# An adaLN block with a spectral filter on one core: turning transfers issued ahead of normalisations, shift weights and tables queued later, special filter rows turned in the row loop, the gather two groups sooner

## Chip, cores and metric

The kernel runs on one core of one Trainium2 chip. The metric is the device time of one execution in microseconds (us), as the median of several runs. Besides the timed runs there is one profiled execution; all places and durations inside the kernel come from that one, counted from the start of its span.

The engines are called PE (matrix multiplications; PEld is its loading of weights), DVE (vector), ACT (scalar), POOL (GpSimd) and SP (it only issues transfers). Each has its own instruction queue and works through it in order; they wait for one another by semaphores. Transfers issued from SP, ACT or POOL are carried out by 16 DMA engines.

## The reference

There are two sub-blocks on x of 2048 x 640, each with a layernorm that is shifted and scaled, and a gated addition. The six modulation vectors come from one row `c`.

```python
mod = (silu(c) @ w_mod).reshape(1, 6, 1, -1)     # w_mod: 640 x 3840
sa, ca, ga, sb, cb, gb = ...                     # its six slices

h = layernorm(x) * (1 + ca) + sa
y = irfft2(rfft2(h) * (w_r + 1j * w_i))          # filter: 2048 x 321, complex
x = x + ga * y
h = layernorm(x) * (1 + cb) + sb
x = x + gb * ((silu(h @ w_gate) * (h @ w_up)) @ w_down)   # hidden width 1728
```

Inputs and output are bf16. The Fourier transform runs over both dimensions, tokens (2048) and features (640).

## The kernel before

The kernel is one long function that writes the instructions out in order; nothing reorders them. The order of the Python lines is the order in each engine's queue. The transforms are done as matrix products with tables of cosines and sines.

**Loads (L260 to L291, on SP).** SP issues x in 128-token tiles (`load_x(i)` brings tiles 2i and 2i+1), the token table `M`, the scale weights `wm_ca`, the feature table `R` (`Rp`), the first half of the filter's rows (`load_w`, L282, into `Wt[:, 0]` for the imaginary and `Wt[:, 2]` for the real part), the shift weights `wm_sa` (L287), the table `Ktab` (L289) and 16 special rows of the filter (`Wrow`, L291). At most eight transfers use the eight semaphores in turn, so an issue waits for the landing of the eighth one before it.

**The turned filter half.** The filter's second half is needed with its rows in reverse order. `flip` (L278), on POOL's queue, copies it from one place in DRAM to another, row by row in reverse; SP loads the result (L465) when that copy has landed. There are two flips, for `A_w_i` (L425, behind the first normalisations) and `A_w_r` (L463, in the row loop at t = 0).

**The row loop (L447 to L482)** runs over t = 0 to 7, each with two token tiles. For a tile, DVE takes mean and variance (`bn`, L325), POOL raises to the power -1/2 (`rstd_of`, L340) and POOL or DVE normalises (`xhat`, L350 on DVE, L352 on POOL; `xpair` does two tiles). Two early tiles have their statistics from ACT (`act_stats`, `act_var`). PE does the token transform (`st_a`, L365), ACT evicts it (L368), PE does the feature transform (`st_b`, L374 and L376) with tables `Rs` that hold the scale 1 + ca (L436 to L443), and ACT or DVE evicts into A (`a_ev`, L380). The loop does the statistics of tiles 2t+6 and 2t+7 while it transforms tile pair t+1. At t = 0 SP's queue receives the two loads of the turned halves, `wm_r` part 0 (the weights of the gate ga, L466), and the tables `Kstab`, `RI` and `Htab` (L467 to L469).

**The shift** enters only few frequencies. `sp_sa` (L387) multiplies the shift weights with silu(c) on PE (25 small matmuls, helper `mod_cols`, L319), DVE copies the result (L390), POOL spreads it (L391 to L394); `sp_sums` (L397) sums it over the features (10 matmuls, L401) and DVE scales it into `SA` (L402). Both stand in the row loop, at t = 6 and t = 7.

**The filter stage (L494 to L765).** The feature frequencies l = 0 to 80 are worked on in 21 groups, most of four. A is transposed once per l: groups 0 to 4 on PE (`t2_pe`, L519), the others by four DMA transposes that SP issues (`t2_dma`, L500) for l = 1 to 15, 16 to 31, 32 to 47 and 64 to 79. Per group PE mixes the row classes (`mix`, L538), DVE multiplies with the filter in two products of three terms each (`prod`, L562), PE combines and turns (`stage_b`, L569), ACT evicts (L572), PE mixes back (`stage_c`, L594), ACT or DVE evicts (`evac`, L603). The middle term needs the sum of real and imaginary filter, which `wsum` (L385) makes on DVE or POOL for a range of columns, for each half of the rows (rk = 0 the direct, rk = 8 the turned half). The loop runs over g; in step g it issues mix and products of group g + 2 and the back end of group g and before.

**The special rows** (frequencies that are a multiple of 128, one row of the transposed groups) go a path of their own: the filter's special rows are reversed (`sp_w(0)`, ACT, L615) and transposed by PE (`sp_w(1)`, L622, copied by ACT, L624, summed by POOL, L625); `sp_gather` (L629, on POOL, at g = 8) collects the special row of all groups and adds `SA`, so it waits for all four DMA transposes; `sp_mm` (L638, L643, L647) and `sp_ev` at g = 10, 12 and 14 mix, multiply and mix back, with `Kstab` as the table. POOL then puts the row into place by two small transfers (L666, L667).

**Behind it** PE does the inverse token transform (`s1em`, L688, with `Htab`, whose second half POOL makes with signs from `Kstab`, L746) and the inverse feature transform (L1220, L1223, with `RI`, which POOL multiplies with the gate ga, L752), and then the second sub-block: L1049 and L1079 for gate and up, L927 and L950 for down.

Of the kernel before, what the change touches and what calls it, by code (L numbers as in the profile page):

```python
# [19 lines left out]
NL = 81  # L20
# [146 lines left out]
def adaln_block_kernel(ctx, tc, A_x, A_w_r, A_w_i, B_x, B_w_gate, B_w_up, B_w_down, c, w_mod, out):  # L167
# [69 lines left out]
    Kstab = rE.cut(32904, [578])  # L237
    wm_sa = rE.cut(34560, [NC5, D])

    psum = ctx.enter_context(tc.tile_pool(name="psum", bufs=1, space=bass.MemoryType.PSUM)).tile([P, 8, 512], F32, name="psum")  # L240
# [40 lines left out]
    def load_w(i, w):  # L281
        nc.sync.dma_start(Wt[:, i, 0:8, :], bass.AP(tensor=w.tensor, offset=w.offset + 321, ap=[[321, P], [256 * 321, 8], [1, 321]]))  # L282

    load_x(4, 4)
    load_w(0, A_w_i)
    load_w(2, A_w_r)
    nc.sync.dma_start(wm_sa[:], wm_v[:, :, 0:D])  # L287
    wm_m = wm_v[:, :, 2 * D:6 * D].rearrange("p k (i d) -> p k i d", i=4)
    nc.sync.dma_start(Ktab[:], K_dram)  # L289
    for i, w in ((0, A_w_i), (1, A_w_r)):  # L290
        nc.sync.dma_start(Wrow[:, i, :], w.rearrange("(k2 k1) l -> k2 k1 l", k1=P)[:, 0, :])  # L291


# [28 lines left out]
    if True:  # L322
# [44 lines left out]
        def ht_ev(t, lo=0, hi=NC5, eng=None):  # L367
            (eng or nc.scalar.copy)(HTs[t % 3][:, lo:hi], zA[:, lo:hi])  # L368
# [18 lines left out]
        def sp_sa():  # L387
            mps = psum[:, 3, 0:NC5]
# [5 lines left out]
            nc.gpsimd.tensor_copy(_rev(SL, 1024, [[1, 4], [132, 2], [16, 8]]),  # L394
                                  sa4[:].unsqueeze(2).unsqueeze(3).to_broadcast([P, 4, 2, 8]))

        def sp_sums():  # L397
            sps = psum[:, 3, 128:128 + NL]
# [13 lines left out]
        bn(1)  # L412
        rstd_of(0, 2)
        nc.vector.tensor_copy(sc_col[:], sc_f[:])
        bn(2)
# [8 lines left out]
        xhat(2, nc.vector)  # L424
        flip(A_w_i, Wflip[0])  # L425
        idle_pe(3)
        idle2(9)
        st_a(0)
        ht_ev(0)
        mps = psum[:, 3, 32:32 + 32 * NC5]  # L430
        mod_cols(mps, wm_ca, range(0, 3), 32)
# [10 lines left out]
        nc.vector.tensor_scalar_mul(Rs[:, 0, 2, :], Rp[:, 2, :], one_p_ca[:, 2:3])  # L442
        nc.vector.tensor_scalar_mul(Rs[:, 0, 3, :], Rp[:, 3, :], one_p_ca[:, 3:4])  # L443
        act_var(5)
        rstd_of(4, 2)
        on_dve = {(4, 1), (5, 1), (6, 1)}
        for t in range(8):  # L447
# [11 lines left out]
            if u < NT:  # L459
                bn(u + 1)  # L460
                rstd_of(u, 2)
                if t == 0:
                    flip(A_w_r, Wflip[1])  # L463
                    for i in range(2):
                        nc.sync.dma_start(Wt[:, 2 * i, 8:16, :], Wflip[i][:])  # L465
                    nc.sync.dma_start(wm_r[:, :, 0, :], wm_m[:, :, 0, :])  # L466
                    nc.sync.dma_start(Kstab[:], Ks_dram)  # L467
                    nc.sync.dma_start(RI[:], RI_dram)
                    nc.sync.dma_start(Htab.rearrange("p (t h) v k -> p t h (v k)", h=2)[:, :, 0, :], H_dram.rearrange("p t v k -> p t (v k)"))  # L469
            for ck in range(2):  # L470
# [7 lines left out]
            if t == 6:  # L478
                sp_sa()
                wsum(48, 64, 0, nc.vector)  # L480
            if t == 7:
                sp_sums()  # L482
        for ls in (slice(0, 48), slice(64, 81)):
# [9 lines left out]
    if True:  # L493
# [14 lines left out]
        t2_dma(2)  # L508
        t2_dma(3)
        nc.sync.dma_start(wm_r[:, :, 1:3, :], wm_m[:, :, 1:3, :])  # L510
        nc.sync.dma_start(wm_r[:, :, 3, :], wm_m[:, :, 3, :])
# [97 lines left out]
        Osp = rE.cut(21192, [80])  # L609
        Wrev = rE.cut(21352, [2, 322], parts=16)  # L610
        Wsp = rE.cut(22640, [3, 2, NT, 2], parts=81)

        def sp_w(part):
            if part == 0:
                nc.scalar.copy(Wrev[:, :, 0:321], _rev(Wrow, 320, [[321, 2], [-1, 321]]))  # L615
            elif part == 1:
                tp = psum[0:81, 3, 448:512].bitcast(BF16).rearrange("p (v h a k) -> p v h a k", v=2, h=2, a=2)
                for v in range(2):
                    for hl in range(2):
                        for a in range(2):  # L620
                            o = 160 * (1 - a if hl else a)
                            nc.tensor.transpose(tp[:, v, hl, a], (Wrev if hl else Wrow)[:, v, o:o + 81], identb[0:16, 0:16])  # L622
                for v in range(2):
                    nc.scalar.copy(Wsp[:, 2 * v].rearrange("p h k a -> p h a k"), tp[:, v])  # L624
                nc.gpsimd.tensor_tensor(Wsp[:, 1], Wsp[:, 0], Wsp[:, 2], ALU.add)  # L625

        def sp_gather():
# [86 lines left out]
        t2_pe(3)  # L714
        xps2 = mix(2)
        prod(2, xps2, 0)
        prod(2, xps2, 1)
        ga_mod(320, 3)
        stage_a(3)
        ga_mod(0, 3)  # L720
        for lo, hi in ((0, 16),):
            wsum(lo, hi, 0, nc.vector)
        sp_w(0)
        for rk in (0, 8):
            v = [_rev(Wt, WP * i + 321 * rk + 80, [[321, 8], [160, 2]]) for i in range(3)]
            nc.gpsimd.tensor_tensor(v[1], v[2], v[0], ALU.add)
        wsum(0, 16, 8, nc.gpsimd)
        sgn_H = Htab.rearrange("p (t h) v k -> p t h (v k)", h=2)
        for g in range(NG + 1):
            for lo, rk in {1: ((16, 0), (16, 8)), 4: ((32, 0), (32, 8)), 9: ((64, 0), (64, 8))}.get(g, ()):  # L730
                wsum(lo, lo + 16, rk, nc.gpsimd)
            if g == 3:
                sp_w(1)
            if g == 5:
                nc.gpsimd.tensor_copy(sgnc[:], Kstab[:, 576:577])
            if g == 8:
                sp_gather()
# [620 lines left out]
```

## Time and profile before

| | us |
|---|---|
| median of 3 timed runs | 253.17 (253.15 to 253.75) |
| profiled execution | 253.96 |
| its span, first to last instruction | 252.2 |
| PE busy in the span | 237.0 (94%) |
| DVE busy | 204.9 (81%) |
| ACT busy | 166.6 (66%) |
| POOL busy | 72.8 (29%) |

The granted clock of PE is 1.0 throughout. Places in time: the first `st_a` starts at 8.62 us, the last at 30.43; the first DMA transpose is issued at 36.25; the products of the filter stage run from 37.70; `s1em` starts at 67.02.

The profile is read from several views. The page gives busy time by engine, the busy share in 40 slices, and the groups of instructions with mean duration and with the idle time before them and what ended it. The chain of waits follows the last instruction back to what released it. The timeline lists instructions in order with start and duration. The windows give the busy time of each engine in a stretch, the granted clock, and in the last two columns the busy share of the DMA engines (it can pass 1, since it is a sum over packets that overlap) and what they moved. In all views `L352` is a line of the kernel before, `psum<-rE` is output and input, and rX, rM, rA, rE, rW, rH, rL and rY are regions of on-chip memory that several tensors share one after the other.

### The profile page before, as it was taken

What the parts mean: (1) busy time and instruction counts of PE and PEld (TensorE: products, weight loads), DVE (VectorE), ACT (ScalarE), POOL (GpSimd) and SP (SyncE); (2) the same over time, 40 slices, a digit from 0 to 9 for tenths busy, and PEclk for the clock granted to TensorE, in tenths of its full rate; (3) what the DMA queues carried; (4) which work ended last, traced back from release to release, by engine and by line L of the source; (5) the groups of instructions that cost most, each with busy time, mean ns of one, the idle gap of its engine ahead of it and who ended that gap; (6) DMA issues with size and microseconds to landing.
All of it is one profiled execution on the core that took longest, in us unless ns stands there. A gap on an engine that the chain in (4) does not pass through costs nothing.

```text
span 252.2 us, 5929 instructions
## 1 busy us (share of the span) xinstructions
PE 237.0 (94%) x2237; PEld 185.8 (74%) x2237; DVE 204.9 (81%) x494; ACT 166.6 (66%) x329; POOL 72.8 (29%) x104
## 2 busy tenths in 40 slices
PE   8668997979999999999999999999999999999994
PEld 3556875969889888778887778888775665656773
DVE  4899668867669999699998996878998788879974
ACT  2867755859689788858965377876247777774220
POOL 5478626576170624102001320000442000003410
PEclk9999999999999999999999999999999999999999
DMA  6999999999999899910002420300611000000111
GB/s 157 381 335 202 291 379 184 182 281 369 250 355 202 251 244 197 191 54 3 1 3 40 86 60 27 56 0 3 105 52 55 0 0 0 4 0 1 55 52 52
DMA packets 41822, 32.51 MB, mean 129 GB/s; under 512 B 21793, under 2 KB 38306, under 8 KB 41794
## 3 DMA queue, kind: packets, MB, share of 16 engines
q1 hardware_dynamic: 39568, 26.50, 41.0%
q0 software_dynamic: 2080, 5.60, 10.5%
q8 instruction: 17, 0.28, 0.5%
q14 instruction: 11, 0.09, 0.1%
q10 hardware_dynamic: 146, 0.04, 0.1%
HBM read 24.80 MB, written 3.94 MB: 114 GB/s over the span
## 4 chain that ended last, share of the span: by engine, by line
PE 77%; DMA 13%; DVE 4%; SPq 2%; issue 2%; ACT 1%; POOL 0%; DVEq 0%; ACTq 0%; POOLq 0%
PE psum L1079 35%; PE psum L950 19%; PE psum L1049 6%; DMA wflip_r<-in_A_w_r_dram 5%; DMA rM<-in_w_mod_dram 3%; PE psum L927 3%; PE psum L688 3%; DMA rL<-rA 2%; DMA rX<-in_A_x_dram 2%; PE psum L1220 2%; PE psum L1223 2%; PE psum L1037 2%; SPq L500 1%; DVE bn6a L325 1%; PE psum L569 1%
## 5 line engine op out<-in xcount | busy, mean ns | idle before, releaser
L1079 PEld LDWEIGHTS <-rW 128*128 128x128 bf16 (+1 forms) x429 | 42.0, 98 | 12.6
L1079 PE MATMUL psum<-rW 128*128 128x256 bf16 (+1 forms) x247 | 42.2, 287 | 0.0
L976 POOL TENSOR_TENSOR rM<-rM,rL 128x320 f32<-128x320 f32 x6 | 5.4, 904 | 96.6 <-ACT rL L975 96.6
L562 DVE TENSOR_TENSOR rM<-psum,rW 128x384 bf16<-128x384 f32 (+2 forms) x42 | 20.5, 543 | 5.7 <-PE psum L538 4.8
L950 PEld LDWEIGHTS <-rE 128*128 128x128 f16 (+1 forms) x196 | 19.0, 97 | 7.8
L950 PE MATMUL psum<-rE 128*128 128x320 f16 (+1 forms) x147 | 22.9, 299 | 0.0
L1117 ACT COPY rX<-psum 128x384 f32<-128x384 f32 (+2 forms) x27 | 14.0, 519 | 7.5 <-PE psum L1079 7.4
L1079 PEld LDWEIGHTS <-rE 128*128 128x128 f16 x156 | 15.3, 98 | 4.7
L1110 ACT COPY rH<-psum 128x384 f32<-128x384 f32 (+2 forms) x27 | 13.9, 516 | 7.0 <-PE psum L1079 6.3
L1114 DVE TENSOR_TENSOR rH<-psum,rM 128x512 bf16<-128x512 f32 (+1 forms) x24 | 15.0, 624 | 4.1 <-PE psum L1079 2.2
L1133 ACT ACTIVATE rL<-psum 128x384 bf16<-128x384 f32 (+2 forms) x27 | 14.4, 532 | 5.5 <-PE psum L1079 3.4
L1118 DVE TENSOR_TENSOR rX<-psum,rX 128x384 f32<-128x384 f32 (+2 forms) x27 | 16.3, 605 | 1.6 <-ACT rX L1117 1.4
L1225 DVE SCALAR_TENSOR_TENSOR rM<-psum,rX 128x640 f32<-128x640 f32 x16 | 13.0, 820 | 4.5 <-ACT rL L692 3.1
L1104 ACT COPY rM<-psum 128x384 f32<-128x384 f32 (+2 forms) x27 | 13.9, 514 | 4.0 <-PE psum L1079 3.9
L365 PE MATMUL psum<-rE 128*128 128x256 bf16 x80 | 10.7, 275 | 5.3 <-POOL rE L352 2.6
L1079 PE MATMUL psum<-rE,rY 128*128 128x256 f16 (+1 forms) x78 | 15.6, 290 | 0.0
L1079 PE MATMUL psum<-rW,rE 128*128 128x256 bf16 (+1 forms) x78 | 15.6, 290 | 0.0
L1134 ACT ACTIVATE rL<-rX 128x384 bf16<-128x384 f32 (+2 forms) x27 | 15.1, 558 | 0.0
L572 ACT CAST rY<-psum 128x512 bf16<-128x512 f32 (+2 forms) x21 | 11.8, 577 | 4.9 <-PE psum L569 4.9
L325 DVE BATCH_NORM_STATS2 bn6a<-rX 128x6 f32<-128x320 bf16 x28 | 12.3, 479 | 3.1 <-DMA rX<-in_A_x_dram 3.1
L1049 PE MATMUL psum<-rW 128*128 128x256 bf16 x130 | 14.5, 273 | 0.0
L919 DVE TENSOR_TENSOR rA<-psum,rM 128x320 bf16<-128x320 f32 (+1 forms) x27 | 12.1, 472 | 2.4 <-PE psum L927 2.3
(231 smaller groups left out, 630.4 us busy)
## 6 DMA issues: line engine op xcount, KB each, us to landing
out_dram<-rA SPq DMA_DIRECT2D x31, 80.0 KB, 1.6
rX<-in_A_x_dram SPq DMA_DIRECT2D x7, 320.0 KB, 7.4
rA<-in_B_w_down_dram SPq DMA_DIRECT2D x2, 960.0 KB, 13.7
rY<-in_B_w_gate_dram POOLq DMA_DIRECT2D x2, 832.0 KB, 7.5
rM<-in_w_mod_dram SPq DMA_DIRECT2D x2, 800.0 KB, 9.8
rM<-in_w_mod_dram SPq DMA_DIRECT2D x1, 1600.0 KB
rW<-in_B_w_gate_dram SPq DMA_DIRECT2D x1, 1440.0 KB, 10.2
rW<-in_B_w_up_dram SPq DMA_DIRECT2D x2, 640.0 KB, 7.4
```

The lines of the kernel that those rows point to most:

```text
L325: nc.vector.bn_stats(bn6a[:, ti % 2, k, :], x_sb[:, ti, 320 * k:320 * k + 320])
L562: nc.vector.tensor_tensor(PPs[g][:, v0:v1, hl], xv[:, v0:v1, hl], in1, ALU.mult)
L950: nc.tensor.matmul(o, lhsT=lhs[rows(k), k], rhs=rhs[rows(k), k], start=start and k == ks[0], stop=stop and k == ks[-1], skip_group_check=True)
L1049: nc.tensor.matmul(gu[u], lhsT=Wgu[:, u, c5, ff * 128:(ff + 1) * 128], rhs=h2T[:, :, c5, :], start=(c5 == 0), stop=(c5 == NC5 - 1))
L1079: nc.tensor.matmul(o[:, f], lhsT=w, rhs=b, start=(start and f == 0 and i == 0), stop=(stop and f == len(groups[g]) - 1 and i == len(ops) - ...
L1104: nc.scalar.copy(c0, X)
L1110: nc.scalar.copy(c2, X)
L1114: nc.vector.tensor_tensor(c11, Z, c0, ALU.add)
L1117: nc.scalar.copy(c3, X)
L1118: nc.vector.tensor_tensor(c22, Y, c3, ALU.add)
L1133: nc.scalar.activation(g21, X, ACT.Silu, scale=-1.0)
L1134: nc.scalar.activation(g22, c22, ACT.Silu, scale=-1.0)
```

## The change

- **Turning transfers.** The flip of `A_w_i` is issued ahead of the second power on POOL, and the flip of `A_w_r` ahead of the normalisation of tile 4. To that end `act_var(5)` and `rstd_of(4, 2)` stand ahead of the scale's eviction. One of the table products with the scale (L443) moves from DVE to ACT.
- **Loads.** x tiles 12 and 13 are issued behind the imaginary filter half, tiles 14 and 15 behind the real one. The shift weights leave SP's queue: POOL issues them in the row loop, at t = 6. `Ktab` goes behind the special rows. `Kstab`, `Htab` and `RI` go behind the four DMA transposes.
- **Special filter rows.** Reversal and transposes move from the filter stage into the row loop, at t = 6 and t = 7; POOL does the reversal and DVE the two copies, where ACT did them.
- **The shift.** `sp_sa` moves behind the products of group 2, and `sp_sums` to g = 1.
- **Filter sums.** Columns 0 to 15 of the turned half go from POOL to DVE. Columns 16 to 31 move from g = 1 to g = 2 and 32 to 47 from g = 4 to g = 6, in each step behind mix and products.
- **Gather.** `sp_gather` moves from g = 8 to g = 6, ahead of the sums of columns 32 to 47. The copy of the signs moves from g = 5 to g = 9.
- `ga_mod(320, 3)` moves ahead of the products of group 2. Places in on-chip memory follow from the above.

```diff
-    load_x(4, 4)
+    load_x(4, 2)
     load_w(0, A_w_i)
+    load_x(6)
     load_w(2, A_w_r)
-    nc.sync.dma_start(wm_sa[:], wm_v[:, :, 0:D])
+    load_x(7)
-    nc.sync.dma_start(Ktab[:], K_dram)
     for i, w in ((0, A_w_i), (1, A_w_r)):
         nc.sync.dma_start(Wrow[:, i, :], ...)
+    nc.sync.dma_start(Ktab[:], K_dram)
...
         rstd_of(0, 2)
+        flip(A_w_i, Wflip[0])
...
         xhat(2, nc.vector)
-        flip(A_w_i, Wflip[0])
         idle_pe(3)
         idle2(9)
         st_a(0)
         ht_ev(0)
+        act_var(5)
+        rstd_of(4, 2)
+        flip(A_w_r, Wflip[1])
...
-        nc.vector.tensor_scalar_mul(Rs[:, 0, 3, :], Rp[:, 3, :], one_p_ca[:, 3:4])
-        act_var(5)
-        rstd_of(4, 2)
+        nc.scalar.mul(Rs[:, 0, 3, :], Rp[:, 3, :], one_p_ca[:, 3:4])
...
                 if t == 0:
-                    flip(A_w_r, Wflip[1])
                     for i in range(2):
                         nc.sync.dma_start(Wt[:, 2 * i, 8:16, :], Wflip[i][:])
                     nc.sync.dma_start(wm_r[:, :, 0, :], wm_m[:, :, 0, :])
-                    nc.sync.dma_start(Kstab[:], Ks_dram)
-                    nc.sync.dma_start(RI[:], RI_dram)
-                    nc.sync.dma_start(Htab...[:, :, 0, :], H_dram...)
+            if t == 6:
+                nc.gpsimd.dma_start(wm_sa[:], wm_v[:, :, 0:D])
+                nc.gpsimd.tensor_copy(Wrev[:, :, 0:321], _rev(Wrow, 320, [[321, 2], [-1, 321]]))
+            if t == 7:
+                sp_w()
...
             if t == 6:
-                sp_sa()
                 wsum(48, 64, 0, nc.vector)
-            if t == 7:
-                sp_sums()
...
         t2_dma(3)
+        nc.sync.dma_start(Kstab[:], Ks_dram)
+        nc.sync.dma_start(Htab...[:, :, 0, :], H_dram...)
+        nc.sync.dma_start(RI[:], RI_dram)
         nc.sync.dma_start(wm_r[:, :, 1:3, :], wm_m[:, :, 1:3, :])
...
         xps2 = mix(2)
+        ga_mod(320, 3)
         prod(2, xps2, 0)
         prod(2, xps2, 1)
-        ga_mod(320, 3)
+        sp_sa()
         stage_a(3)
         ga_mod(0, 3)
...
-        sp_w(0)
...
-        wsum(0, 16, 8, nc.gpsimd)
+        wsum(0, 16, 8, nc.vector)
         for g in range(NG + 1):
-            for lo, rk in {1: ((16, 0), (16, 8)), 4: ((32, 0), (32, 8)), 9: ((64, 0), (64, 8))}.get(g, ()):
-                wsum(lo, lo + 16, rk, nc.gpsimd)
-            if g == 3:
-                sp_w(1)
-            if g == 5:
+            if g == 1:
+                sp_sums()
+            if g == 9:
                 nc.gpsimd.tensor_copy(sgnc[:], Kstab[:, 576:577])
-            if g == 8:
+            if g == 6:
                 sp_gather()
             if 1 < g < NG - 2:
                 ...
                 stage_a(g + 2)
                 ...
+            for lo, rk in {2: ((16, 0), (16, 8)), 6: ((32, 0), (32, 8)), 9: ((64, 0), (64, 8))}.get(g, ()):
+                wsum(lo, lo + 16, rk, nc.gpsimd)
```

The new `sp_w` holds the two parts of the old one but for the reversal, with the copies on DVE:

```python
def sp_w():
    tp = psum[0:81, 3, 384:448].bitcast(BF16).rearrange("p (v h a k) -> p v h a k", v=2, h=2, a=2)
    for v in range(2):
        for hl in range(2):
            for a in range(2):
                o = 160 * (1 - a if hl else a)
                nc.tensor.transpose(tp[:, v, hl, a], (Wrev if hl else Wrow)[:, v, o:o + 81], identb[0:16, 0:16])
    for v in range(2):
        nc.vector.tensor_copy(Wsp[:, 2 * v].rearrange("p h k a -> p h a k"), tp[:, v])
    nc.gpsimd.tensor_tensor(Wsp[:, 1], Wsp[:, 0], Wsp[:, 2], ALU.add)
```

More of the change, by code (lines that the diff above doesn't have):

```diff
@@ L238, in adaln_block_kernel @@
     wm_sa = rE.cut(34560, [NC5, D])
+    Wrev = rE.cut(18464, [2, 322], parts=16)
+    Wsp = rE.cut(34064, [3, 2, NT, 2], parts=81)
     psum = ctx.enter_context(tc.tile_pool(name="psum", bufs=1, space=bass.MemoryType.PSUM)).tile([P, 8, 512], F32, name="psum")
@@ L387, in sp_sa @@
         def sp_sa():
-            mps = psum[:, 3, 0:NC5]
+            mps = psum[:, 5, 448:448 + NC5]
             mod_cols(mps, wm_sa)
@@ L395, in sp_sa @@
                                   sa4[:].unsqueeze(2).unsqueeze(3).to_broadcast([P, 4, 2, 8]))
+        def sp_w():
+            tp = psum[0:81, 3, 384:448].bitcast(BF16).rearrange("p (v h a k) -> p v h a k", v=2, h=2, a=2)
+            for v in range(2):
+                for hl in range(2):
+                    for a in range(2):
+                        o = 160 * (1 - a if hl else a)
+                        nc.tensor.transpose(tp[:, v, hl, a], (Wrev if hl else Wrow)[:, v, o:o + 81], identb[0:16, 0:16])
+            for v in range(2):
+                nc.vector.tensor_copy(Wsp[:, 2 * v].rearrange("p h k a -> p h a k"), tp[:, v])
+            nc.gpsimd.tensor_tensor(Wsp[:, 1], Wsp[:, 0], Wsp[:, 2], ALU.add)
         def sp_sums():
-            sps = psum[:, 3, 128:128 + NL]
+            sps = psum[:, 3, 384:384 + NL]
             for i in range(10):
@@ L466, in adaln_block_kernel @@
                     nc.sync.dma_start(wm_r[:, :, 0, :], wm_m[:, :, 0, :])
-                    nc.sync.dma_start(Kstab[:], Ks_dram)
-                    nc.sync.dma_start(RI[:], RI_dram)
-                    nc.sync.dma_start(Htab.rearrange("p (t h) v k -> p t h (v k)", h=2)[:, :, 0, :], H_dram.rearrange("p t v k -> p t (v k)"))
+            if t == 6:
[3 more added lines that the diff above has]
+                sp_w()
             for ck in range(2):
@@ L509, in adaln_block_kernel @@
         t2_dma(3)
+        nc.sync.dma_start(Kstab[:], Ks_dram)
+        nc.sync.dma_start(Htab.rearrange("p (t h) v k -> p t h (v k)", h=2)[:, :, 0, :], H_dram.rearrange("p t v k -> p t (v k)"))
+        nc.sync.dma_start(RI[:], RI_dram)
         nc.sync.dma_start(wm_r[:, :, 1:3, :], wm_m[:, :, 1:3, :])
@@ L609, in adaln_block_kernel @@
         Osp = rE.cut(21192, [80])
[L610 to L625, printed above, removed]
         def sp_gather():
```

## Prediction

> **What bounds the kernel now.** First the page's busy slices (40 of 6.3 us): PE shows 9 from slice 11 on, and the chain of waits runs over PE almost alone from 67.02 us, where `s1em` starts (L688), to 248.87. What moves `s1em` moves the end; after it I cost nothing. So I read the chain of waits, in order of time, before that (start, length, what):
>
> ```profile
> 17.11 13.17 DMA wflip_r<-in_A_w_r_dram
> 30.29 0.34 SPq L465
> 30.68 8.55 DMA rM<-in_w_mod_dram
> 39.28 0.87 PE psum L672 x5
> ...
> 40.61 1.10 SPq L500
> 41.76 2.64 SPq L500
> 44.44 5.79 DMA rL<-rA
> ...
> 52.28 0.81 POOL rE L629 x5
> 53.13 0.30 PE psum L638 x3
> ```
>
> From 17 to 52 us the chain is transfers: the turned half of `A_w_r`, `wm_r`, then the four DMA transposes (L500), which the gather (L629) and the special matmuls (L638) wait for. The timeline of SP's queue shows how they were issued:
>
> ```profile
> 14.02 8.08 SPq L287 DMA_DIRECT2D rE<-in_w_mod_dram  x1
> ...
> 36.25 11.38 SPq L500 DMA_TRANSPOSE rL<-rA  x3
> 47.80 2.90 SPq L500 DMA_TRANSPOSE rM<-rA  x1
> ```
>
> SP stands 8 us in the issue of the shift weights `wm_sa`, and 5.46 in the first transpose (36.25 to 41.71, the longest in the answer on L500; the others take 2.6 to 3.2). Both stand behind a full queue. The windows of 2 us show it in their last two columns (DMA share, GB/s; before them PE, PEld, DVE, ACT, POOL, clock):
>
> ```profile
> 20.00:22.00 2.00, 1.93 (x20) 1.58 (x18) 1.90 (x8) 1.21 (x2) 1.58 (x3) 1.00 1.09 269
> 24.00:26.00 2.00, 1.86 (x18) 1.41 (x16) 1.65 (x7) 2.00 (x3) 1.75 (x3) 1.00 1.28 111
> 32.00:34.00 2.00, 2.00 (x41) 1.83 (x40) 1.61 (x4) 0.98 (x2) 0.01 (x1) 1.00 1.00 395
> 40.00:42.00 2.00, 1.82 (x23) 1.49 (x22) 1.97 (x6) 0.90 (x3) 1.71 (x3) 1.00 0.54 44
> ```
>
> The engines are full to 40 us; the queue then drains and the transposes begin. Last, DVE's timeline in the filter stage (in brackets the wait before):
>
> ```profile
> 44.85 0.82 DVE L562 TENSOR_TENSOR rM<-psum,rW 128x288 bf16<-128x288 f32 x2 [1.24 <-PE psum L538]
> 46.15 5.76 DVE L562 TENSOR_TENSOR rM<-psum,rW 128x384 bf16<-128x384 f32 x12 [0.47 <-PE psum L538]
> 53.80 1.02 DVE L562 TENSOR_TENSOR rM<-psum,rW 128x384 bf16<-128x384 f32 x2 [1.89 <-PE psum L538]
> ```
>
> DVE's products (42, some 0.49 each) are this stage's work; the 1.89 is group 12 waiting for the gather. Where this waits, the change acts.
>
> **1. Turning transfers early.** On POOL the first flip moves from 11.58 into the idle 6.3 to 9.5 (POOL waits there for L339); the second from 17.11 to about 12.4, behind the power for tiles 4 and 5. Each costs POOL 1.39 and 1.33. Behind the second stood the tile-6 normalisation: ready at 17.4 (L343), it ran at 18.49, and PE waited 0.98 for it. That is gone, but DVE runs without a gap from 13.62 to 22.8, so the row loop gains at most some 0.7 (L443 to ACT 0.17, no stretched L339 at 18.85 0.3, two waits of 0.26 for POOL). `act_var(5)` ahead of L434 delays that by 0.5; L443's move and the earlier bn(6) give it back.
>
> The price is in the queue. By the windows 1.63 MB have moved by 8 us and 5.26 by 18; x, `M`, `wm_ca` and `R` are 4.70 (DMA issues: 4586 KB). After the change x tiles 14 and 15 stand behind `w_i` and `w_r`, with both flips running beside. From 8 us: 3.07 MB at 375 GB/s (mean of 8 to 16) 8.2 us, then 4 x 642 KB = 2.63 MB at 270 (18 to 22) 9.7: landed at 25.9. Bounds: 23.5 if the second flip falls behind (2.4 less), 29.4 if these tiles land where `w_r` lands today (11.48 + 17.9). Their bn starts at 24.40 now. (Tiles 6 and 7, landed by 13.1 today, may slip too, by at most the quarter that the flip takes; that slip ends inside this wait.) From it to the last `st_a`: bn to L343 1.4, two L352 1.73, L340 0.69, hand-over 0.36, L352 0.94: 5.1. So 31.0 against 30.43: **+0.6**, bounds -0.7 and +4.1.
>
> By the Trainium skill ("DMA: Bandwidth & Descriptors", Queues, rings and completion order) every engine takes turns between the queues, packet by packet; this would let the flips (as many rows as `w_i` and `w_r` together) finish ahead of x, and is the slow rival below. The trace bears it out only partly: of the 2.1 MB moved from 12 to 18 us the first flip got at most 0.56 (5.26 - 4.70), a quarter.
>
> **2. End of the row loop.** PE loses the 25 shift matmuls (0.93) and ten sums (0.56, waited 0.17), gains 8 small transposes (0.48, L622's price). That buys little: st_b(7) waits for DVE's L380, ending 33.82. DVE no longer waits 0.44 for the sums ahead of the last evictions, nor does L402 there; it gains two copies, bounded by 0.34 (L624 on ACT, both) and hidden ahead of 34.75, where it waits. A is ready 0.6 earlier: 35.65. POOL does the reversal (0.72 on ACT, L615; 0.7 to 1.4 taken) after issuing `wm_sa` (up to 1.4): it is done at 32.5 to 33.2, and PE needs it at 33.2 (32.57 + 0.6); if it slips, the loss is that slip. With +0.6 from part 1 the first transpose starts at 36.25, as now.
>
> **3. Lighter queue.** Kstab, RI and H (976 KB, 1.0 MB) leave the queue ahead of the transposes: 2.6 us at 390 GB/s. `wm_sa` stays ahead of them, on POOL's queue. So the first issue ends at 39.1 (41.71 - 2.6); bounds 38.9 (36.25 + 2.7) and 41.7. The other three as now (9.0): 48.1; landed 1.3 later, 49.4; gather 0.97: 50.4 (now 53.07). The waits for the turned half (0.63 DVE, 2.08 POOL) and `wm_r` (0.89 PE) go too.
>
> Kstab is now issued after the last transpose, at 48.1. Its landing: 2.4 us (first x load, empty queue) to 8.5 (today's). The queue ahead is empty but for that transpose, so I take 2.5: 50.6, later than the gather. L638 at 50.7: **-2.4**. By the same page (Anatomy of one DMA) a transfer costs about 2.0 us plus its bytes, an estimate of 2.3 for Kstab's 144.5 KB; no other term uses it.
>
> **4. DVE and POOL in the filter stage.** DVE's products start about 37.45 (now 37.70: the 0.63 gone, +0.6, less the 0.15 of t2_pe). Then 3.83, sa_col 0.16, four filter sums 1.6 (two moved from POOL), SA 0.24: group 4 at 43.3, its 0.98, group 5's 0.82, twelve products 5.76: free at 50.9 (now 51.91). So group 12 waits 0.5 for L638 and starts at 51.4. ACT's 0.72 and 0.34 and PE's 0.48 leave groups 2 and 3, which is why group 5 no longer waits 1.24.
>
> On POOL the gather now stands ahead of the sums for columns 32 to 47: 4 x 0.69 = 2.75, ready at 53.15. Group 13 needs them at 52.7, so DVE waits 0.4: 53.15 against 55.13, **-2.0**. Behind it: sums 64 (56.0; group 17 needs them at 57.9), the H signs 2.2 (58.2), the two row-127 DMAs, landing 6.1 and 6.4 after issue, 64.3 and 65.3; `s1em` needs the first at 65.0, L697 the second at 66.9. `wm_r` 1 and 2 (1.64 MB) go 1 us sooner but behind 1.0 MB: 48.1 + 6.8 at 390 GB/s, landed about 57, needed at 58.2 (L551). These margins, 0.7 to 2 us, are the cover that a larger gain would use up.
>
> **Sum.** -2.0. Profiled: 253.96, of which 252.2 is span and 1.76 lies around it; so 250.2 + 1.76 = 251.96. The median shown, 253.17, is 0.79 lower; I carry the difference: 253.17 - 2.0 = **251.2**.
>
> **Rivals.**
> - **All early** (0.17): x keeps pace (landed by 24.4), the queue drains with it, the first issue ends at 37.7; L638 at 49.3, group 13 at 51.75: -3.4, 249.8. For it: the flip got only a quarter. Against: the 111 GB/s at 24 us.
> - **Shift weights late** (0.10): issued by POOL about 31, landing 7.5 to 9.6 later (POOL's L858 group and its like), 14 as the flips. At 40.6 PE stands before `sp_sa`, `sa_col` comes at 41.6 instead of 40.35, DVE is free at 52.15, group 13 at 53.5: 251.5. At 45 DVE would be free at 56.4, 2.6 past group 12's start today.
> - **x late, slower** (0.13): tiles 14 and 15 land at 29.4, like `w_r` today. Row loop +4.1, first transpose at 39.75, its issue ends 42.45, last landed 52.75, gather 53.7, group 13 at 56.5: +1.4, 254.6. It decides from a landing at about 28.1 (counted back from group 13 at 55.13: gather 52.4, last landed 51.4, first transpose at 38.4, last `st_a` at 33.2); below that the change gains. For it: today's `w_r`, the slow windows, SP's 8 us issue.
> - **Little moves** (0.10): landing near 27.5, or Kstab taking 4.5 us, within 0.7 of now: 253.
>
> **Chances.** Forecast 0.50 (250.3 to 252.2); the four cases take the rest. A measurement tells some 0.3% (0.76 us) from no change. Faster: 0.50 + 0.17 + 0.10, less 0.02 for shift weights very late: 0.75; same 0.11; slower 0.14. The range leaves out the slow rival and the far end of the early one: 249.3 to 253.7.
>
> **What would show it.** SP's `wm_sa` block of 8 us gone; first transpose issue under 3 us, last transpose landed near 49.4; L638 near 50.7 and behind it a DVE wait below 0.6 for group 12; a wait of group 13 for POOL's sums. Wrong if DVE's bn of tiles 14 and 15 waits for x beyond 28.1, if PE stands at the shift matmuls beyond 41, or if L638 waits for Kstab beyond 53.

## The result and the profile after

The changed kernel takes **256.91 us** (median of 4 runs, 256.26 to 257.78), the kernel before beside it 253.26: ratio 1.0142, 95% interval 1.0105 to 1.0179. That is slower by 3.65 us, where 251.2 was forecast and 249.3 to 253.7 given as the range. The profiled execution took 257.78, its span is 256.0.

Lines have moved: after, `bn` is L328, `xhat` L353 (DVE) and L355 (POOL), `st_a` L368, the first transposes L513, the gather L628, `sp_mm` L637, `s1em` L687. DVE's timeline of the row loop (start, length, instruction, in brackets the wait before it and what ended it):

```profile
14.73 0.88 DVE L328 BATCH_NORM_STATS2 bn6a<-rX 128x6 f32<-128x320 bf16 x2
...
21.33 0.89 DVE L328 BATCH_NORM_STATS2 bn6a<-rX 128x6 f32<-128x320 bf16 x2 [5.27 <-DMA rX<-in_A_x_dram]
...
22.38 0.10 DVE L346 SCALAR_TENSOR_TENSOR nmean<-mv,rstd 128x2 f32<-128x2 f32 x1
22.40 0.44 DVE L353 TENSOR_SCALAR rE<-rX,mv,rstd 128x640 bf16<-128x640 bf16 x1
```

The line at 21.33 is `bn(8)`: DVE stood 5.27 us for tile 8, whose statistics ran at 16.28 without a wait in the kernel before. It stood at the head of DVE's queue, and the two lines behind it belong to tiles 6 and 7, which had long landed: the loop writes `bn(u)`, then `xpair(u - 2)`. So one late tile also held the tiles ahead of it. PE's timeline shows what that did to the row groups, first before, then after:

```profile
19.42 1.28 PE L365 MATMUL psum<-rE 128*128 128x256 bf16 x10 [0.98 <-POOL rE L352]
22.07 1.51 PE L365 MATMUL psum<-rE 128*128 128x256 bf16 x10
...
30.43 1.25 PE L365 MATMUL psum<-rE 128*128 128x256 bf16 x10
```

```profile
23.65 2.33 PE L368 MATMUL psum<-rE 128*128 128x256 bf16 x10 [5.51 <-POOL rE L355]
28.14 1.82 PE L368 MATMUL psum<-rE 128*128 128x256 bf16 x10
...
36.57 1.25 PE L368 MATMUL psum<-rE 128*128 128x256 bf16 x10
```

The fourth group (tiles 6 and 7) starts 4.23 us late, and the last 6.14: another 1.9 were lost on the way. The ten matmuls of the fourth group take 2.33 instead of 1.28. The windows of 2 us say why (last three columns: granted clock, DMA share, GB/s):

```profile
18.00:20.00 2.00, 0.13 (x2) 0.00 (x0) 0.00 (x0) 1.37 (x3) 0.00 (x0) 1.00 1.08 146
22.00:24.00 2.00, 0.35 (x2) 0.30 (x3) 1.90 (x9) 0.00 (x0) 0.94 (x1) 0.62 1.13 292
24.00:26.00 2.00, 2.00 (x11) 1.37 (x9) 1.93 (x8) 0.00 (x0) 1.38 (x2) 0.50 1.01 274
28.00:30.00 2.00, 2.00 (x14) 1.55 (x13) 1.90 (x6) 0.70 (x1) 1.95 (x3) 0.68 1.05 415
```

After PE had stood, its granted clock fell to half and came back near 29.3. Behind the row loop the change did what it was costed for. SP's timeline, against the lines of 14.02 and 36.25 before:

```profile
9.85 7.51 SPq L257 DMA_DIRECT2D rX<-in_A_x_dram  x1
17.41 0.52 SPq L284 DMA_DIRECT2D rW<-in_A_w_r_dram  x1
17.97 4.48 SPq L257 DMA_DIRECT2D rX<-in_A_x_dram  x1
...
41.59 6.96 SPq L513 DMA_TRANSPOSE rL<-rA  x3
48.73 3.35 SPq L513 DMA_TRANSPOSE rM<-rA  x1
```

SP's block of 8 us at `wm_sa` is gone, but a block of 7.51 now stands in the issue of x itself. The first three transposes take 6.96 instead of 11.38. They start 5.34 late; `sp_mm` starts 2.89 late (56.02), `s1em` 3.45 late (70.47), and the span is 3.8 longer.

### The profile page after: what moved, and what is told of

The parts are those of the page before. It is cut to its first block, busy times and chain, and to the rows that moved or that the text cites. A ratio compares the mean times of both kernels' runs of the same rounds, so it can differ in the third digit from the quotient of the medians.

```text
span 256.0 us, 5928 instructions
## 1 busy us (share of the span) xinstructions
PE 239.9 (94%) x2237; PEld 187.5 (73%) x2237; DVE 205.2 (80%) x497; ACT 166.6 (65%) x327; POOL 72.5 (28%) x104
## 4 chain that ended last, share of the span: by engine, by line
PE 83%; DMA 5%; DVE 3%; issue 3%; ACT 2%; SPq 1%; POOL 1%; DVEq 0%; ACTq 0%
PE psum L1078 35%; PE psum L949 18%; PE psum L1048 6%; DMA rM<-in_w_mod_dram 4%; PE psum L368 4%; PE psum L926 3%; PE psum L687 3%; PE psum L1219 2%; DMA rX<-in_A_x_dram 2%; PE psum L1222 2%; PE psum L1036 2%; ACT rE L371 1%; PE psum L585 1%; PE psum L554 1%; PE psum L377 1%
## 5 line engine op out<-in xcount | busy, mean ns | idle before, releaser
L368 PE MATMUL psum<-rE 128*128 128x256 bf16 x80 | 11.9, 302 | 8.3 <-POOL rE L355 6.4
L328 DVE BATCH_NORM_STATS2 bn6a<-rX 128x6 f32<-128x320 bf16 x28 | 12.3, 480 | 7.9 <-DMA rX<-in_A_x_dram 7.9
L368 PEld LDWEIGHTS <-rE 128*128 128x128 bf16 x80 | 9.0, 118 | 10.7 <-POOL rE L355 6.9
L371 ACT CAST rE<-psum 128x1280 bf16<-128x1280 f32 (+1 forms) x8 | 9.4, 1169 | 11.3 <-PE psum L368 11.3
```

Of the source, the lines that this page charges most:

```text
L368: nc.tensor.matmul(zA[:, c5], lhsT=lhsT, rhs=Mtab[:, t, h], start=(h == 0), stop=(h == 1))
```

## Experiments

**Theory A**: the early flips slow the loads of `M` and x down, tiles 8 and 9 come late, DVE and PE stand, the clock falls. **Theory B**: the new order of the loads does it. In the table: the waits for x tiles from tile 6 on (each until when), the starts of the last `st_a`, the first transpose and `s1em` in the profiled execution, and the ratio to the kernel before, measured beside each (its medians were 253.2 to 253.5). Places come from one execution each; verdicts from the ratios. An interval that leaves out 1 tells a kernel from the kernel before.

| kernel | tiles waited for, until | last `st_a` | transpose | `s1em` | ratio, 95% interval |
|---|---|---|---|---|---|
| before | none | 30.43 | 36.25 | 67.02 | 1 |
| after | 8: 21.33 | 36.57 | 41.59 | 70.47 | 1.0142, 1.0105 to 1.0179 |
| e1_flips_back | 12: 25.37, 14: 29.51 | 35.24 | 40.25 | 69.49 | 1.0118, 1.0082 to 1.0155 |
| e2_x_first | 6: 13.69 (0.64 long), 8: 20.80 | 35.75 | 40.77 | 70.11 | 1.0102, 1.0057 to 1.0147 |
| e3_only_flips_early | 8: 21.45 | 36.12 | 41.94 | 69.81 | 1.0141, 1.0096 to 1.0185 |
| e4_warm_pe | 8: 21.38 | 35.49 | 40.50 | 69.60 | 1.0109, 1.0078 to 1.0140 |
| e5_both_back | none | 29.44 | 34.45 | 65.31 | 0.9974, 0.9950 to 0.9998 |
| e6_only_x_order | 12: 25.39, 14: 29.52 | 35.37 | 41.17 | 69.42 | 1.0103, 1.0063 to 1.0142 |
| e7_tables_back | none | 29.80 | 34.82 | 66.60 | 1.0011, 0.9985 to 1.0037 |
| e8_flip_r_early | none | 29.02 | 34.04 | 66.81 | 0.9991, 0.9965 to 1.0017 |
| e9_wm_r0_first | none | 29.86 | 34.87 | 64.77 | 1.0000, 0.9966 to 1.0034 |
| e10_ga_later | none | 30.01 | 35.02 | 65.20 | 0.9999, 0.9974 to 1.0023 |
| e11_warm_ga | none | 29.47 | 34.49 | 66.12 | 0.9981, 0.9960 to 1.0002 |
| e12_flip_i_early | 8: 19.87 | 33.96 | 38.98 | 67.97 | 1.0091, 1.0056 to 1.0126 |
| e13_wm_r0_warm | none | 30.22 | 35.23 | 68.76 | 1.0076, 1.0047 to 1.0104 |
| e14_half_flip_i | 8: 18.22 | 32.31 | 37.33 | 66.51 | 1.0002, 0.9976 to 1.0029 |
| e15_best | none | 29.28 | 34.87 | 69.52 | 1.0162, 1.0120 to 1.0204 |
| e16_sa_behind_r0 | none | 29.59 | 34.61 | 64.74 | 0.9967, 0.9944 to 0.9990 |
| e17_sa_old_place | none | 29.77 | 35.05 | 65.22 | 0.9971, 0.9945 to 0.9997 |
| e18_loads_as_before | none | 29.70 | 37.51 | 67.00 | 1.0002, 0.9976 to 1.0028 |

### What makes the row loop stand

**e1_flips_back**, against the changed kernel:

```diff
         rstd_of(0, 2)
-        flip(A_w_i, Wflip[0])
...
         xhat(2, nc.vector)
+        flip(A_w_i, Wflip[0])
...
-        flip(A_w_r, Wflip[1])
...
                 if t == 0:
+                    flip(A_w_r, Wflip[1])
```

> The changed kernel with both flips put back where they were before (flip_i behind the normalisations of the first four tiles, flip_r after the last row load's address work at t = 0); everything else as changed. Theory A (the early flips take about half of the DMA engines while the middle matrix and the x tiles 8 and 9 are loading, tiles 8 and 9 arrive about 5 us late, the row loop stands, and the TensorE clock falls after the idle stretch): the fourth row group starts near 19.4 again instead of 23.65, the clock stays at 1.00, the first transpose is issued near 36 and the time falls to 250.5 to 251.5, below the kernel before. Theory B (the order of the loads does it, the row loads of w_i and w_r standing among the x tiles): tiles 8 and 9 stay late and the time stays near 256.

**e2_x_first**, against the changed kernel:

```diff
-    load_x(4, 2)
+    load_x(4, 4)
     load_w(0, A_w_i)
-    load_x(6)
     load_w(2, A_w_r)
-    load_x(7)
```

> The changed kernel with all four last pairs of x tiles ahead of the row loads of w_i and w_r, as before; the flips stay early. Theory A: tiles 8 and 9 stood ahead of those loads already and are as late as in the changed kernel (wait of their statistics until 20 to 22), so the time stays at 256 to 257. Theory B: the x tiles are back in time and the time falls to about 251.

Neither theory alone holds. Each of the two, undone by itself, left the time where it was (256.41 and 256.56), since the other remained. With the flips late, tiles 8 and 9 came in time, the fourth group started at 18.74, and then tiles 12 and 14 were late, as DVE's timeline of e1_flips_back shows:

```profile
25.37 0.89 DVE L328 BATCH_NORM_STATS2 bn6a<-rX 128x6 f32<-128x320 bf16 x2 [4.31 <-DMA rX<-in_A_x_dram]
29.51 0.89 DVE L328 BATCH_NORM_STATS2 bn6a<-rX 128x6 f32<-128x320 bf16 x2 [1.69 <-DMA rX<-in_A_x_dram]
```

**e3_only_flips_early** is the kernel before with the flips at the places of the change, and with the small steps that go with the second one (`act_var(5)`, `rstd_of(4, 2)` and one scaling on ACT). **e6_only_x_order** is the kernel before with the new order of `load_x` and `load_w`. **e5_both_back** is the changed kernel with the edits of e1 and e2 together.

> The kernel before with both flips early (and the two small statistics steps and the ScalarE scaling that go with the second), nothing else of the change. Theory A: the row loop alone loses what the changed kernel lost there, 5 to 6 us at the first transpose (36.25 to about 41.5 to 42.5), the clock falls near 24, and since the tables stay in the row loop nothing is won back behind it: 257 to 260. Theory B: the x tiles are loaded first here, so nothing is late: 253 to 254.

> The kernel before with the new order of loads alone (x tiles 12 and 13 behind w_i, 14 and 15 behind w_r). Theory C: tiles 12 and 13 are waited for until about 25 and 14 and 15 until about 29.5, as with the flips put back; the idle stretch brings the clock down for a few us; the first transpose is issued near 41 and, since the tables and the first transpose's queue stay as before, nothing is won back: 256.5 to 258.5. If the order of the loads costs nothing by itself: 253 to 254.

> The changed kernel with both undone: the flips at their old places and all x tiles ahead of the row loads of w_i and w_r. The first runs split the loss: with the flips early tiles 8 and 9 are late (until 21), with the flips late and the new order of the loads tiles 12 to 15 are late (until 25.4 and 29.5). Theory C (either of the two edits alone makes the row loop stand, and nothing else of the change costs anything there): no statistics step waits for an x tile after the first three groups, the last row group starts at 30 to 31, the clock stays at 1.00, and the 2 to 2.7 us that the filter stage wins back in the changed kernel now stand alone: 250.5 to 251.3. Theory D (something else of the change, the transfers on POOL's queue or the rows turned in the row loop, costs there too): the first transpose stays later than 37, 252.5 to 255.

These settle the place. The early flips (with those small steps) cost the kernel before 1.4%, the order alone 1.0%, and they don't add: while the loop stands for tile 8, the later tiles land. With both undone no tile is waited for and the loss is gone. But theory C's gain came out at 0.26% (0.7 us), below the 2 to 2.7 us expected; that is the second question.

**e12_flip_i_early** and **e8_flip_r_early** move one flip alone in e5_both_back; **e14_half_flip_i** moves half of the first:

```diff
         rstd_of(0, 2)
+        flip(A_w_i, Wflip[0], 0, 4)
...
-        flip(A_w_i, Wflip[0])
+        flip(A_w_i, Wflip[0], 4, 4)
```

> The kernel with both undone, and the first flip alone issued early (at about 6); the second stays late. With the second flip alone early the time was 253.1, no different from both late. If the loss of the early flips is the first flip's, which is in flight while the middle matrix and the tiles 8 and 9 load, tiles 8 and 9 are waited for until 20 or later, the fourth row group starts after 22, the clock falls, and the time is 255 to 257. If it takes both flips in flight at once to make them late, the wait is under 2 us and the time 252.5 to 254.

> As the kernel with both undone, but the second flip (of w_r) is issued early, at about 12, as in the changed kernel; the first is issued at its old place, a little ahead of it. If what hurts is a flip in flight while x tiles are still loading, this hurts less than the first flip's move, because only tiles 12 to 15 are still to come: a wait of 0.5 to 2 us there, 251 to 253. If two flips together take more than half of the DMA engines, tiles 12 and 13 wait until 24 or later: 254 to 256.

> Both edits undone, and half of the first flip (half of its rows, 321 of 642 KB) issued early, the other half at the old place. With none early tiles 8 and 9 are not waited for; with all early (second flip late) they are waited for until 19.87. If the flip delays the loads by the packets it sends while they are in flight, half of it delays them by about half: statistics of tiles 8 and 9 at 16 to 18, with a wait of 0.5 to 2.5, and a time of 253 to 254.5. If it is the flip's being there at all (turns between queues, whatever its size), the wait is as long as with the whole: until 19.5 to 20.5, 255 to 256.

It is the first flip. Issued at 6.15 it cost 0.9%, the second at 12.81 nothing that can be measured. The wait for tile 8 grows with the bytes that go early: none, then until 18.22 with 321 KB, 19.87 with 642, 20.80 to 21.45 with both flips. This fits a delay by the packets beside the loads better than one by the flip's mere presence; the other half of e14's flip was in flight from its old place, so the steps aren't clean doses.

**e4_warm_pe**, against the changed kernel:

```diff
-                idle2(6 if t == 0 else 1)
+                idle2({0: 6, 2: 46}.get(t, 1))
```

> The changed kernel with 46 more idle matmuls on TensorE in the stretch in which it stands before the fourth row group; their results are used by nothing. If the fall of the granted clock to 0.5 comes from that idle stretch, the clock stays near 1.00 between 22 and 30, the last row group follows the fourth by about 11 us (as before) instead of 13, and the time falls by 1.5 to 2, to about 255. If the fall has another cause (the load of the DMA engines, say), the clock falls all the same and the time stays at 256 to 257 or more.

The clock stayed at 1.00 (0.997 or more in all four executions, against 0.984 to 0.993 in the changed kernel), so the fall comes from PE's stand. The fourth group started as late as in the changed kernel (23.70), and the last followed it by 11.79 us instead of 12.92: in the profile the fall costs 1.1. The time came down by 0.3% of the kernel before, but the intervals of the two ratios overlap, so the profile shows this size and the timed runs don't. Part of the rest went into waits for tiles 12 and 14 (0.36 and 0.54), which a slower loop had covered.

### Why the rest gives so little

**e7_tables_back** loads the three tables in the row loop again, in e5_both_back.

> As the kernel with both undone, but the three tables of the filters and the inverse transform (Kstab, RI, Htab) are also loaded in the row loop again, ahead of the transposes. If the gain of the filter stage is that of the lighter queue (the first three transposes land sooner), the first transposes take 9 to 11.5 us again instead of 7 and most of the gain goes: 252 to 253. If it comes from the work moved between the engines (special rows, gather, shift weights), the time stays within 0.5 of the kernel with both undone.

The transposes took 11.25 instead of 8.80 and the gain was gone. In e5_both_back itself, the row loop ended sooner, and PE then stood for another load (PE's timeline, then windows of 1 us with the clock in the third column from the end):

```profile
38.80 1.19 PE L669 MATMUL psum<-rM,sc_rep 128*128 128x320 bf16 x5 [1.80 <-DMA rM<-in_w_mod_dram]
```

```profile
37.00:38.00 1.00, 0.00 (x0) 0.00 (x0) 1.00 (x4) 0.31 (x1) 0.00 (x0) 1.00 1.13 57
40.00:41.00 1.00, 1.00 (x27) 0.86 (x25) 0.17 (x1) 0.42 (x1) 0.00 (x0) 0.50 1.14 213
42.00:43.00 1.00, 1.00 (x12) 0.71 (x10) 0.97 (x4) 0.20 (x1) 0.17 (x3) 0.71 1.12 209
```

That load is `wm_r` part 0. Three kernels, all from e5_both_back, go at it: e9 issues it ahead of the turned rows, e10 moves its product behind the products of group 2, e11 keeps PE busy ahead of it.

```diff
+                    nc.sync.dma_start(wm_r[:, :, 0, :], wm_m[:, :, 0, :])
                     for i in range(2):
                         nc.sync.dma_start(Wt[:, 2 * i, 8:16, :], Wflip[i][:])
-                    nc.sync.dma_start(wm_r[:, :, 0, :], wm_m[:, :, 0, :])
```

> The kernel with both undone, and the load of the first modulation columns (wm_r, column block 0) issued ahead of the two loads of the turned filter rows instead of behind them. There TensorE stood 1.80 us for that load at 38.8, the granted clock fell to 0.50 from 39.6 to 42.6, and the first 0.4 per cent of gain was what stayed. If that wait and the clock are where the rest of the gain went, the wait is gone, the clock stays at 1.00 over 36 to 44, and the time falls by 1.5 to 2.5, to 250.5 to 251.5. If the row loads that now land later become late in its place, the time stays at 252.5 to 253.5.

> The kernel with both undone, and the first part of the gate's modulation (TensorE's product with wm_r) put back behind the products of the third group, where it stood before the change. VectorE's products of that group then no longer wait for anything, but TensorE waits for the same load all the same, and has nothing else to do there: TensorE's wait and the fall of the clock stay, and the time stays within 0.5 of the kernel with both undone (252.4 to 253.4). If the earlier place of that product is what makes the wait, the time falls to 251 to 252.

> The kernel with both undone, and 14 idle matmuls on TensorE ahead of the product that waits for wm_r (their results are used by nothing). If the fall of the clock to 0.5 comes from the idle time before it, the clock stays at 1.00 from 38 to 43, and the time falls by about 1 (3 us at half speed, of which part is waiting), to 251.7 to 252.2; the wait for the load itself stays. If the clock falls nevertheless: 252.9 or more.

e9 lost the wait in the profile (DVE waited 0.94 for the turned rows instead), and the median stayed at that of the kernel before (253.43 against 253.48). e10 still waited 1.3 us for the load, and gained nothing either. e11 kept the clock up as expected (0.997 or more in all twelve executions), and its gain over e5 is too small to measure. So the fall of the clock alone isn't what took e5's gain. **e13_wm_r0_warm** joins e9 and e11, and **e15_best** adds the early second flip.

> Both edits undone, the wm_r load ahead of the row loads, and 14 idle matmuls ahead of the product that uses it (results unused). With the load ahead alone the profiled execution had a span of 250.3 and no wait for that load, but the median did not fall: of 12 executions eight had a mean granted clock of 0.993 or less and took 253.2 to 255.2, the three with 1.000 took 251.4 to 252.7. With the idle matmuls alone all twelve had 0.997 to 1.000. If the missing gain is the clock falling in the stand behind the row loop, nearly all executions now have 0.997 or more and the median is 251.2 to 252.2 (0.5 to 0.9 per cent under the kernel before). If the slower executions have another cause, the clock is 1.00 and the times stay spread up to 255, median 253.

> As the kernel with wm_r ahead and idle matmuls, and also the second flip early (at about 12.5), which by itself made no tile late and let the row loop end 0.4 sooner. If the turned rows' landing now bounds the end of the row loop and the products, 250.7 to 252; if not, the same as without (within 0.4).

Both are slower, against the expectation. DVE's timeline of e13:

```profile
39.06 0.52 DVE L386 TENSOR_TENSOR rW<-rW 128x256 bf16<-128x256 bf16 x2 [3.10 <-DMA rW<-wflip_r]
39.49 2.88 DVE L576 TENSOR_TENSOR rM<-psum,rW 128x384 bf16<-128x384 f32 x6
```

With `wm_r` ahead, the turned rows are late: the first sum waits 3.10 us for them, and the products start at 39.49 instead of 35.62 (e5). The idle matmuls couldn't help, since they waited 2.80 us for these products themselves, and the clock fell again. The order of the loads is that of e9, where the same wait was 0.94; why it was longer here isn't shown. In these profiles the loads that are due at the end of the row loop (turned rows, `wm_r`, `wm_sa`) trade places: with one put first, another is waited for.

**e16_sa_behind_r0** issues `wm_sa` on SP's queue behind `wm_r`; **e17_sa_old_place** behind `load_w(2, A_w_r)`, as before the change; **e18_loads_as_before** is e17 with the tables in the row loop as well, so that of the change only engine work is left, and `Ktab` one place later in the queue.

> Both edits undone, and the shift weights (wm_sa, 800 KB) issued on SP's queue right behind wm_r instead of on POOL's queue at the same time. Same bytes, about the same moment, one queue instead of two. If the wait for wm_r at the end of the row loop (1.80 us) comes from the two loads running side by side, wm_r now lands 2 to 4 us sooner, TensorE does not wait for it, the clock stays at 1.00; but the first transposes stand behind wm_sa in the same queue and may take 9 to 11 us again. By the first part alone 251 to 252; if the transposes' delay takes it back, 252.5 to 253.5. The last trials of moving a load ahead cost more than they brought because the turned rows became late; here the turned rows stay ahead.

> Both edits undone, and wm_sa loaded early, behind w_r, where it was before the change. If the later load of the shift weights is what takes the gain (it meets wm_r at 29), wm_r lands by 35 to 37, no wait, clock 1.00; the tables stay late, so the first transposes land sooner as well: 251 to 252. If the stream of loads is simply full from 5 to 39 and the 800 KB delay the turned rows by about 2 us instead, the row loop's end and the products are later by 1 to 2 and the time stays 252.5 to 253.5.

> All the loads at the places and in the order of the kernel before (flips, x tiles, wm_sa, tables); of the change only the moves of engine work are left: special rows turned in the row loop, shift weights' product and sums later, gather two groups sooner, scalings moved between engines. If the gain came from these (1.8 us wait for the gather gone, row loop shorter by the work moved out of it), 251.5 to 252.5; if it came from the lighter queue, 253 to 254.

In e16 `wm_r` was no longer waited for (PE waited 0.7 for `wm_sa` instead), with clock 1.00 and `s1em` at 64.74; its 0.9967 is the best of all runs, below the kernel before, but its interval overlaps those of e5 and e17. The place of `wm_sa` makes no difference that can be told. Tables late against tables in the row loop is 0.9974 against 1.0011 (e5, e7) and 0.9971 against 1.0002 (e17, e18): 0.3 to 0.4% both times, though the intervals within each pair overlap a little. So what the change wins, it wins with the tables. The engine moves without the loads show no gain (1.0002), but e18 doesn't price them free of new waits: in e18 PE also waits in the row loop for the special rows' load and reversal (its waits: what waited for what, us in total, times, longest):

```profile
PE psum L405 <- POOL rE L484: 0.8, 1, 0.8
PE psum L405 <- DMA rE<-in_A_w_i_dram: 0.8, 1, 0.8
```

Not settled: why the median of e9 stays at 253.43 when its profiled execution took 252.11. Of its twelve executions four had a mean granted clock of 0.998 or more and took 251.43 to 252.66, the profiled one among them; eight had 0.993 and took 253.19 to 255.18. Half speed for 3.41 us, as in the profile of e13, would lower the mean of some 252 us by 0.7% (an estimate), so one fall fits the eight; of them there is no trace. Single profiles can mislead about gains: that of e16 (251.18) is its lowest of twelve times, that of the kernel before (253.96) lies above its median. What making the loop safe against a late tile would give (`xpair(u - 2)` ahead of `bn(u)`) is open too; that wasn't tried.

## Why the prediction was wrong

**Step 1 failed.** It put the row loop at +0.6, at most +4.1; it was +6.14 at the last `st_a`. Three sentences of it were wrong.
- It looked at tiles 14 and 15, behind `w_i` and `w_r`. In the changed kernel tile 8 came first, late behind `M` with the first flip beside it; `M` landed 11.9 us after issue (7.7 before). The order that it priced is real too, and shows where the loop isn't already held for tile 8: without the early flips tile 14 was waited for until 29.5 (e1, e6), where the sum had 25.9 and 29.4 as its bound, and tile 12, which it didn't price, until 25.4.
- It let earlier tiles slip "by at most the quarter that the flip takes". The quarter was counted over 12 to 18 us. By the view of the DMA queues of the kernel before, POOL's queue (q0, which carries the flips) moved nothing until 16.6, five us after the first flip's issue; from then on it had 34, 40, 59 and 67% of the bytes in the four windows of 2 us up to 24. Its lines for 16 to 18 us (packets, MB, share of the engines' time; q1 is SP's queue), first before, then after:

```profile
q1 hardware_dynamic: 556, 0.40, 72.6%
q0 software_dynamic: 179, 0.21, 40.7%
```

```profile
q0 software_dynamic: 91, 0.28, 57.3%
q1 hardware_dynamic: 275, 0.21, 49.1%
```

After, the flips flow from 10.8 us on, and from 12 to 20 had 34 to 63% of the bytes for 37 to 55% of the engines' time. With the engines full (share 1.01 to 1.15) the total rate also fell, from 341 to 405 GB/s between 8 and 14 us to 146 between 18 and 20. So SP's queue, in which tile 8 stood, moved 1.18 MB from 12 to 20 where it had moved 2.18. What lowers the total rate isn't separated: rows of `w_i` were in flight beside the flips, and in e12, with one packet of POOL's from 18 to 20, SP's queue moved no more than 227 GB/s.

The rule of the Trainium skill that it weighed ("DMA: Bandwidth & Descriptors", Queues, rings and completion order) says that each engine takes turns between queues, packet by packet. It was set aside for that quarter; shares near a half and waits that grow with the early bytes (e14, e12, e3) go with the rule, though no run here shows the turns themselves, and the share isn't fixed (64 to 89% of the bytes for POOL's queue in e8, 16 to 22 us).

- "That slip ends inside this wait" overlooked DVE's order: `bn(8)` stands ahead of the normalisation of tiles 6 and 7. And nothing in it foresaw the clock, 1.1 us of the loss (by e4) and at most 1.9.

By the profiles, step 1 and the shift that follows from it are 5.3 of the 5.8 us between forecast (-2.0) and span (+3.8): the first transpose was 5.34 late where 0 was forecast.

**Step 2 was right in size**: the stretch from the last `st_a` to the first transpose is 0.80 shorter (5.82 to 5.02); 0.6 was forecast.

**Step 3 was right in size in the changed kernel, in part by luck**: from the transpose to `sp_mm` it won 2.45 (5.34 late, then 2.89), forecast 2.4. But the queue had drained by then because the loop was late: 0 GB/s from 34 to 36. With the loop in time (e5), the first three transposes take 2.58 less than before, but PE stood for `wm_r` and ran at half speed meanwhile, and came to `sp_mm` without a wait: 1.75 sooner than before, no more than the 1.80 by which the first transpose is. `Kstab`, taken at 2.5, landed 3.1 after its issue in the changed kernel and held nothing up (the 2.3 beside it in the prediction comes from a section of the Trainium skill on transfers that POOL issues; SP issued this one).

**Step 4** named its margins: the wait for POOL's sums at group 13 didn't come (group 13's products follow directly at 58.03), and 0.56 of the gain is given back between `sp_mm` and `s1em` (2.89 to 3.45 late). New there are waits of DVE for PE (0.21) and ACT (0.38) and of PE for `wm_r` (0.20); which of them costs it isn't shown. DVE also waits 0.71 at 63.01, by the view for POOL's H signs; but it waits as long at the same product in the kernel before (59.93), with no releaser named, so this is no margin used up.

**The rivals.** The slow one had the mechanism's family right (x late), with the wrong tiles and the price of 254.6 too low by 2.3. Its sign for failure, a wait of tiles 14 and 15 beyond 28.1, didn't come in the changed kernel and would not have shown the cause; in e1 and e6, without the early flips, it came (29.5).

## What to carry over

When a transfer is issued sooner, ask what is in flight at that moment and which of it is waited for next; take its share of the queue from the windows in which its packets move, not from a mean that starts before the first of them. In a queue that works in order, a late operand holds back ready work behind it: read the program order at the wait. When a stretch gets shorter, look for the load that is due at its new end before counting the gain. A profile is one execution: hold its time against the median before reading a gain off it.

## What the runs showed of the hardware

With the ends worked out from windows of half a microsecond, the windows around the fall in e5_both_back are (PE busy is the second figure, the clock the third from the end):

```profile
35.76:39.17 3.41, 1.59 (x18) 1.12 (x16) 2.74 (x6) 1.38 (x2) 0.00 (x0) 1.00 1.26 185
39.17:42.58 3.41, 3.41 (x38) 2.40 (x37) 1.23 (x4) 0.42 (x1) 1.12 (x5) 0.50 1.14 221
42.58:46.00 3.42, 3.35 (x58) 3.21 (x57) 2.74 (x9) 2.57 (x5) 0.41 (x1) 1.00 1.54 184
```

Half speed lasted 3.41 us there, in e1 and in e13, and twice that, 6.82, in the changed kernel (22.47 to 29.29, PE busy 2.23 of the first 3.41) and in e8 (2.98 of the first 3.41). In the 3.41 us ahead of the fall PE had been busy for 0.00 (after), 0.93 (e13), 1.25 (e1) and 1.59 (e5). But the busy time of any such stretch doesn't decide alone: in the kernel before, 6.20 to 9.61 had 1.29, with a stand of 2.06 us in it, and the clock stayed at 1.00. The Trainium skill ("TensorE: Matmul & The Clock Gate", Part 1) gives a free-running window of 3413 ns after which an idle PE goes to half rate; the length agrees, and where such windows lie no view here shows, so the threshold stays open. That only a gap beyond 3.4 us does it, as the Trainium skill has it further on the same page, doesn't hold: in e5 PE stood for no longer than 1.80 us.
